# New planned latencies and six more matmuls on zeros in an attention and expert kernel with a planned order

## The chip, the cores and the metric

The kernel runs on one core of a Trainium2 chip. The metric is the device time of one execution in microseconds; the lower the better. Before the change three runs took 217.77, 216.84 and 217.11 us, a median of 217.11 us.

## What is computed

Two branches on the same 2048 x 512 input x, blended by a gate (cut from the reference; B = 1, S = 2048, D = 512):

```python
g = sigmoid((x * gate_w).sum(-1, keepdims=True))
# A: attention, 32 heads of 16, each query sees itself and the 255 keys before it
qkv = (x @ wqkv).reshape(B, S, 3, 32, 16).transpose(2, 0, 3, 1, 4)
scores = einsum("bhqd,bhkd->bhqk", q, k) * 16 ** -0.5
scores = where((i - j >= 0) & (i - j < 256), scores, -1e9)
a = einsum("bhqk,bhkd->bhqd", softmax(scores), v).transpose(0, 2, 1, 3).reshape(B, S, D) @ wo
# B: the 8 tokens with the largest r go through a gated feed-forward layer
r = x @ w_r;  idx = argsort(-r)[:8];  x_sel = x[idx]
y = ((silu(x_sel @ w_gate) * (x_sel @ w_up)) @ w_down) * sigmoid(r[idx])
b = x.at[idx].add(y)
out = g * a + (1 - g) * b
```

w_gate and w_up are 512 x 1792, w_down is 1792 x 512. All inputs are bf16.

## The kernel before

**Tiling.** The 32 heads are four groups c of eight, the 2048 keys four blocks qb of 512. That gives 16 steps s = 4c + qb. A step's scores are 16 key tiles of 32 keys by up to 288 queries, written as one stream of columns and cut into blocks of 512 columns. Such a block, for two halves of 64 partitions, is called a unit here; there are 136. For each unit TensorE writes scores into one of two PSUM pairs (`L717`), ScalarE takes the exponential into P (`L731`), and VectorE clears what lies outside the window (`L752`, for every second unit). TensorE then multiplies P by the values, which stand next to a column of ones in `Vbd` (`L771`), so that the sum of the exponentials comes out beside the result.

**The normalization of a step.** VectorE copies the two PSUM banks to `OXY` (`L800`), which frees the banks. Four small transfers bring the sums to `Dc` (`L805`), VectorE takes their reciprocal (`L812`), a transfer writes it to memory (`fs_r`, `L813`), another reads it back spread over the partitions (`f_Rb`, `L814`), and GpSimd multiplies (`L815`) into OT. `OXY` has three buffers, `Dc` and `Rb` two. The last two steps do it with transposes on TensorE instead (`norm_t`, `L823` to `L848`).

**Around it.** Projections of Q and K (`L582`) and of V (`L606`) are spread between the units. V goes to memory (`fs_v`, `L618`) and is read back in the layout of `Vbd` (`L622`). The routing scores come from `L860`, the feed-forward layer is `L896` to `L958`; its three weights follow each other in the same buffer `f_WF` (`L532`, `L913`, `L942`, each some 1.6 to 1.8 MB), and its result is scattered into a copy of x in memory (`fs_xc`), of which the last group of heads reads its residual (`resid`, `L629` and `L633`). The output product is `L663`, and `L650` with `L656` for the last block of rows.

**What sets the order.** The program is a list of operations with what they read and write. `Sched.schedule` plays it through with an estimated duration for each and, for each transfer, an estimated latency `lat` (2200 ns where none is given). At every step each engine takes, of its operations that are ready by these estimates, the one of the best priority. The result is a fixed order for each engine; on the chip every engine runs its list strictly in that order and waits at an instruction whose inputs are late. Nearly all transfers are issued by SyncE, in one such list. PSUM banks 4 to 7 are handed out in the same play-through. The estimate of when an input is there is this:

```python
if d.dma:
    x = d.t1 + d.lat + 100.0
elif sem:
    x = d.t1 + (70.0 if d.eng == op.eng else self.SEM) + (60.0 if d.eng == "pe" else 0.0)
```

At the head TensorE multiplies zeros into the eight banks (`L539`) while the input is on its way.

## Time and profile before

| | |
|---|---|
| median of three runs | 217.11 us |
| profiled execution | 218.79 us, of it 216.1 us from the first to the last instruction |
| TensorE busy | 169.8 us (79%) |
| VectorE busy | 145.6 us (67%) |
| ScalarE busy | 128.7 us (60%), of it 126.7 us in the 136 exponentials |
| GpSimd busy | 26.4 us (12%) |
| mean granted TensorE clock | 0.906 |

The shares are means over stages that differ: in the middle of the program all engines stand still together several times. The times of the profiled execution add up to its own 218.79 us, which is 1.68 us above the median. Where an engine waits, the trace names the instruction whose semaphore came last, and that is not always where the delay began.

### The profile page before, as it was taken

What the parts mean: (1) busy time and instruction counts of PE and PEld (TensorE: products, weight loads), DVE (VectorE), ACT (ScalarE), POOL (GpSimd) and SP (SyncE); (2) the same over time, 40 slices, a digit from 0 to 9 for tenths busy, and PEclk for the clock granted to TensorE, in tenths of its full rate; (3) what the DMA queues carried; (4) which work ended last, traced back from release to release, by engine and by line L of the source; (5) the groups of instructions that cost most, each with busy time, mean ns of one, the idle gap of its engine ahead of it and who ended that gap; (6) DMA issues with size and microseconds to landing.
All of it is one profiled execution on the core that took longest, in us unless ns stands there. A gap on an engine that the chain in (4) does not pass through costs nothing. (4 is left out here: it accounts for less than half of the span.)

```text
span 216.1 us, 6692 instructions
## 1 busy us (share of the span) xinstructions
PE 169.8 (79%) x2884; PEld 85.9 (40%) x2884; DVE 145.6 (67%) x365; ACT 128.7 (60%) x142; POOL 26.4 (12%) x42
## 2 busy tenths in 40 slices
PE   6699978999059938529898876998988898799930
PEld 1545535444025413215543633653443554534310
DVE  8289999782086398344754758376896866798870
ACT  2019999799017929708283494789969999500000
POOL 8300000100200202022003000202102022220000
PEclk9799999999655988967999996799999999999985
DMA  7997967497965617931477567256121213203841
GB/s 163 237 232 177 208 145 153 90 317 231 249 266 156 258 40 215 245 84 52 141 171 189 133 229 150 55 173 136 55 79 33 79 34 80 72 36 118 294 146 35
DMA packets 53058, 32.17 MB, mean 149 GB/s; under 512 B 37736, under 2 KB 49276, under 8 KB 52992
## 3 DMA queue, kind: packets, MB, share of 16 engines
q1 hardware_dynamic: 51376, 31.16, 53.7%
q10 hardware_dynamic: 1584, 0.52, 1.1%
q8 instruction: 23, 0.38, 0.7%
q14 instruction: 11, 0.09, 0.2%
q0 software_dynamic: 64, 0.02, 0.0%
HBM read 20.20 MB, written 9.42 MB: 137 GB/s over the span
## 5 line engine op out<-in xcount | busy, mean ns | idle before, releaser
L731 ACT ACTIVATE f_P<-f_ps 128x1024 bf16<-128x1024 f32 (+1 forms) x136 | 126.7, 1058 | 55.8 <-PE f_ps L717 29.6
L717 PE MATMUL f_ps<-f_QT,f_Kst 64*128 64x288 bf16 (+5 forms) x744 | 55.1, 252 | 9.8 <-ACT f_P L731 9.2
L771 PE MATMUL f_ps<-f_P,f_Vbd 64*34 64x288 bf16 (+8 forms) x1408 | 48.2, 262 | 4.6 <-DVE f_OXY L800 2.5
L752 DVE TENSOR_TENSOR f_P<-f_P,f_MK 128x512 bf16<-128x512 bf16 (+4 forms) x102 | 37.6, 388 | 15.5 <-ACT f_P L731 15.0
L582 PE MATMUL f_ps<-f_XT,f_W 64*128 64x512 bf16 x256 | 38.9, 389 | 3.0 <-DMA f_XT<-in_A_x_dram 2.4
L717 PEld LDWEIGHTS f_ps<-f_QT,f_Kst 64*128 64x128 bf16 x744 | 22.7, 96 | 41.3 <-ACT f_P L731 34.0
L771 PEld LDWEIGHTS f_ps<-f_P,f_Vbd 64*34 64x34 bf16 x1408 | 27.5, 98 | 27.1 <-issue 16.4
L815 POOL TENSOR_TENSOR f_OT<-f_OXY,f_Rb 128x512 bf16<-128x512 f32 x14 | 17.8, 1270 | 134.3 <-DMA f_Rb<-fs_r 134.3
L606 PE MATMUL f_ps<-f_W,f_XT 64*128 64x256 bf16 x256 | 22.0, 305 | 8.0 <-DVE f_zbf L925 6.4
L812 DVE RECIPROCAL f_RC<-f_Dc 128x32 f32<-128x32 f32 x14 | 4.9, 348 | 23.6 <-DMA f_Dc<-f_OXY 23.6
L800 DVE COPY f_OXY<-f_ps 128x512 f32<-128x512 f32 x28 | 18.3, 681 | 2.9 <-PE f_ps L771 2.9
L596 DVE TENSOR_SCALAR f_Kst<-f_Kr,f_hm 128x512 bf16<-128x512 bf16 x64 | 18.5, 345 | 0.0
L606 PEld LDWEIGHTS f_ps<-f_W,f_XT 64*128 64x128 bf16 x256 | 13.2, 106 | 13.0 <-DVE f_zbf L925 6.7
L582 PEld LDWEIGHTS f_ps<-f_XT,f_W 64*128 64x128 bf16 x256 | 11.0, 96 | 11.1 <-issue 3.5
L613 DVE CAST f_Vn<-f_ps 128x512 bf16<-128x512 f32 x16 | 10.7, 685 | 6.9 <-PE f_ps L606 6.8
L592 DVE CAST f_Kr<-f_ps 128x512 bf16<-128x512 f32 x16 | 10.9, 682 | 5.5 <-PE f_ps L582 5.5
L663 PE MATMUL f_ps<-f_wo,f_OT 64*128 64x512 bf16 x96 | 11.9, 378 | 0.2
L637 DVE SCALAR_TENSOR_TENSOR f_outt<-f_ps,f_g_f,f_xr 128x512 bf16<-128x512 f32 x16 | 11.2, 742 | 0.9 <-PE f_ps L663 0.9
L587 DVE CAST f_QT<-f_ps 128x512 bf16<-128x512 f32 x16 | 10.9, 681 | 0.0
L909 PE MATMUL f_ps<-f_WF,f_xselT 128*32 128x448 bf16 x32 | 2.8, 484 | 10.2 <-DVE f_Kr L592 10.2
L633 DVE TENSOR_SCALAR f_xr<-f_xr,f_omg_f 128x512 bf16<-128x512 bf16 x16 | 4.9, 348 | 5.0 <-DMA f_xr<-fs_xc 5.0
L1031 ACT COPY f_sg<-f_ones_f 1x1 f32<-1x1 f32 x1 | 0.2, 190 | 10.7 <-DVE flag L1027 10.7
(87 smaller groups left out, 75.4 us busy)
## 6 DMA issues: line engine op xcount, KB each, us to landing
fs_v<-f_Vn SPq DMA_DIRECT2D x8, 608.0 KB, 4.2
f_Vbd<-fs_v SPq DMA_DIRECT2D x32, 144.0 KB, 4.7
f_Rb<-fs_r SPq DMA_DIRECT2D x14, 256.0 KB
f_xr<-fs_xc SPq DMA_DIRECT2D x4, 512.0 KB
out_dram<-f_outt SPq DMA_DIRECT2D x16, 128.0 KB
f_OXY<-f_OXY SPq DMA_DIRECT2D x28, 64.0 KB, 2.8
f_WF<-in_B_w_gate_dram SPq DMA_DIRECT2D x1, 1792.0 KB
f_WF<-in_B_w_up_dram SPq DMA_DIRECT2D x1, 1792.0 KB
```

What stands on the lines that cost most here:

```text
L582: return e.matmul(ps[:, bk.i, :], W[R, k, f0:f0 + 128], XT[R, k, 512 * tc:512 * tc + 512], start=first, stop=last, tile_position=(64 * h, ...
L587: S.add("dve", lambda e: e.tensor_copy(out=QT[:, c % 2, 512 * tc:512 * tc + 512], in_=ps[:, bk.i, :]), r=[("bk", id(bk))], w=[("QT", c % 2 ...
L596: S.add(eng, lambda e, j=j: e.tensor_scalar(out=Kst[:, s, :, j, :], in0=Kr[:, n % 2, :].rearrange("p (a k) -> p a k", k=32), scalar1=hm[:, ...
L606: return e.matmul(ps[:, bk.i, 256 * i:256 * i + 256], XT[R, kc, 128 * a:128 * a + 128], W[R, kc, 1024 + 256 * cp:1024 + 256 * cp + 256], s ...
L637: S.add("dve", lambda e: e.scalar_tensor_tensor(out=outt[:, a % 4, :], in0=ps[:, bk.i, :], scalar=g_f[:, a:a + 1], in1=xr[:, (a // 4) % 2, ...
L663: return e.matmul(ps[:, bk.i, :], OT[R, k, 128 * a:128 * a + 128], wo[R, k, :], start=first, stop=last, tile_position=(64 * h, 0), skip_gr ...
L717: ins = e.matmul(ps[:, sbk + v, so:so + m], Kst[R, ks, t, :, :].rearrange("p j k -> p (j k)"), QT[R, c % 2, q0:q0 + m], start=True, stop=T ...
L731: S.add("act", lambda e, p0=p0, n=n, sbk=sbk: e.activation(out=P[:, g, :, p0:p0 + n], in_=ps[:, sbk:sbk + 2, 0:n], func=ACT.Exp, scale=0.2 ...
L752: S.add("dve", lambda e, v=v, m=m: e.tensor_tensor(out=v, in0=v, in1=m, op=ALU.min), r=rd, w=[("M", g, r_[3]) for r_ in b], dur=60 + 2 * k ...
L771: ins = e.matmul(ps[64 * v:64 * v + 34, bk.i, q0:q0 + n], Vbd[R, cp, kh, 36 * q:36 * q + 34], P[R, g, v, PADW + o:PADW + o + n], start=fir ...
L800: S.add("dve", lambda e, b=b, bk=bk: e.tensor_copy(out=OXY[:, x, b, :], in_=ps[:, bk.i, :]), r=[("O", id(bX))], w=[("OXY", x, b, p) for p ...
L815: S.add("pool", lambda e: e.tensor_tensor(out=OT[:, c, 512 * qb:512 * qb + 512], in0=OXY[:, x, 0, :], in1=Rb[:, y, :], op=ALU.mult), r=[(" ...
```

## The change

It changes numbers that the planner reads, and the list of matmuls on zeros. Nothing is computed otherwise, and no operation but the six matmuls is added or removed.

```diff
-                        x = d.t1 + (70.0 if d.eng == op.eng else self.SEM) + (60.0 if d.eng == "pe" else 0.0)
+                        x = d.t1 + (70.0 if d.eng == op.eng else self.SEM) + ((160.0 if op.eng == "pe" else 60.0) if d.eng == "pe" else 0.0)
...
-        for b in list(range(8)):
+        for b in list(range(8)) + [4, 5, 6, 7, 4, 5]:
             S.add("pe", lambda e, b=b: e.matmul(ps[:, b, :], zb[:, 0:128], zb, start=True, stop=True), r=[("xr", 0)], w=[("warm", b)] + ([("S", b // 2)] if b < 4 else []), dur=430, prio=0,
...
                     S.dma(lambda e: e.dma_start(vs[cp, 512 * tc:512 * tc + 512, :].rearrange("(i p) f -> p i f", p=128), Vn[:, s2]),
-                          r=[("Vn", s2, 0), ("Vn", s2, 1)] + [("Vn1", s2, j) for j in range(4)], w=[("vs", cp, tc)], prio=14)
+                          r=[("Vn", s2, 0), ("Vn", s2, 1)] + [("Vn1", s2, j) for j in range(4)], w=[("vs", cp, tc)], prio=14, lat=4500)
                         S.dma(lambda e, j=j, rj=rj: e.dma_start(Vbd[32 * j:32 * j + 32, cp, 16 * tc:16 * tc + 16, :],
                                                                 vs[cp, 512 * tc:512 * tc + 512, rj:rj + 144].rearrange("(a k) f -> k a f", k=32)),
-                              r=[("vs", cp, tc)], w=[("Vbd", cp, tc, j)], prio=14)
+                              r=[("vs", cp, tc)], w=[("Vbd", cp, tc, j)], prio=14, lat=4500)
             S.dma(lambda e: e.dma_start(xr[:, g], xc[512 * qb:512 * qb + 512, :].rearrange("(i p) f -> p i f", p=128)), r=["xc"],
-                  w=[("xr", g)] + [("xu", g, i) for i in range(4)], prio=30)
+                  w=[("xr", g)] + [("xu", g, i) for i in range(4)], prio=30, lat=6000)
...
         def pv_step(s):
             c, qb = s // 4, s % 4
+            LD = 7000 if s < 12 else 3000
...
                     S.dma(lambda e, h=h, b=b: e.dma_start(Dc[64 * h + 32 * b:64 * h + 32 * b + 32, y, :], OXY[32 + 64 * h:34 + 64 * h, x, b, :]),
-                          r=[("OXY", x, b, "d")], w=[("Dc", y, h, b)], prio=10)
+                          r=[("OXY", x, b, "d")], w=[("Dc", y, h, b)], prio=10, lat=LD)
...
-            S.dma(lambda e: e.dma_start(Rb[:, y, :], bass.AP(rs.tensor, s * 4096, [[512, 8], [0, 16], [1, 512]])), r=[("rs", s)], w=[("Rb", y)], prio=10, lat=3200)
+            S.dma(lambda e: e.dma_start(Rb[:, y, :], bass.AP(rs.tensor, s * 4096, [[512, 8], [0, 16], [1, 512]])), r=[("rs", s)], w=[("Rb", y)], prio=10, lat=LD + 1000)
...
-            S.dma(lambda e: e.dma_start(gz[:], gs.rearrange("(a p) -> p a", p=128), allow_slow_non_contiguous=True), r=["gs"], w=["gz"], prio=40, lat=4000)
+            S.dma(lambda e: e.dma_start(gz[:], gs.rearrange("(a p) -> p a", p=128), allow_slow_non_contiguous=True), r=["gs"], w=["gz"], prio=40, lat=9000)
```

From `pv_step` on, lines of the changed kernel are one higher (`L812` becomes `L813`).

What that does to the orders is shown at three places. VectorE, from the copies of step 1 to its reciprocal, before:

```order
L800 COPY f_OXY<-f_ps 128x512
L752 TENSOR_TENSOR f_P<-f_P,f_MK 128x2x4x64
L800 COPY f_OXY<-f_ps 128x512
L592 CAST f_Kr<-f_ps 128x512
L752 TENSOR_TENSOR f_P<-f_P,f_MK 128x2x4x64
L596 TENSOR_SCALAR f_Kst<-f_Kr,f_hm 128x16x32 x2
L752 TENSOR_TENSOR f_P<-f_P,f_MK 128x2x64
L596 TENSOR_SCALAR f_Kst<-f_Kr,f_hm 128x16x32 x2
L587 CAST f_QT<-f_ps 128x512
L752 TENSOR_TENSOR f_P<-f_P,f_MK 128x2x32 x7
L812 RECIPROCAL f_RC<-f_Dc 128x32
L752 TENSOR_TENSOR f_P<-f_P,f_MK 128x2x4x64 x2
```

VectorE in the changed kernel, the last rows up to the reciprocal of the same step; its copies (`L801`) stand 25 and 23 rows of this list ahead of it:

```order
L871 TENSOR_SCALAR f_eg<-f_eg 128x16
L901 CAST f_xselT<-f_ps 128x128
L872 RECIPROCAL f_g_f<-f_eg 128x16
L884 CAST f_sgf<-f_sgb 1x8
L873 CAST f_g_bf<-f_g_f 128x16
L874 CAST f_g_f<-f_g_bf 128x16
L752 TENSOR_TENSOR f_P<-f_P,f_MK 128x2x4x64
L875 TENSOR_SCALAR f_omg_bf<-f_g_bf 128x16
L877 CAST f_omg_f<-f_omg_bf 128x16
L752 TENSOR_TENSOR f_P<-f_P,f_MK 128x2x4x64
L592 CAST f_Kr<-f_ps 128x512
L813 RECIPROCAL f_RC<-f_Dc 128x32
```

Between the second copy and the reciprocal stand 15 instructions before and 31 now; the reciprocal has moved behind the first two masks of step 4. Counted in units whose masks stand ahead, the later copy and the reciprocal of steps 0 to 5 stand after 17 and 22, 29 and 34, 38 and 43, 42 and 47, 49 and 56, 63 and 67 units before, and after 15 and 27, 27 and 38, 38 and 47, 45 and 58, 52 and 63, 63 and 68 now. The first eight operations on the residual (`L633`) stand after 72 to 77 units before and 85 to 95 now.

SyncE where the first feed-forward weight (`f_WF<-in_B_w_gate_dram`) and the sums of the first steps are moved, before:

```order
L532 DMA f_WF<-in_B_w_gate_dram 128x4x1792
L618 DMA fs_v<-f_Vn 128x4x608
L813 DMA fs_r<-f_RC 128x32
L515 DMA f_W<-in_A_wqkv_dram 128x4x256
L622 DMA f_Vbd<-fs_v 32x16x144
L814 DMA f_Rb<-fs_r 128x1x512
L622 DMA f_Vbd<-fs_v 32x16x144 x3
L885 DMA f_sigT<-f_sgf 8x1x1
L805 DMA f_Dc<-f_OXY 32x1x32 x4
```

SyncE at the same place in the changed kernel:

```order
L869 DMA f_gz<-fs_g 128x16x1
L532 DMA f_WF<-in_B_w_gate_dram 128x4x1792
L806 DMA f_Dc<-f_OXY 32x1x32 x4
L622 DMA f_Vbd<-fs_v 32x16x144 x4
L618 DMA fs_v<-f_Vn 128x4x608
L515 DMA f_W<-in_A_wqkv_dram 128x4x128
L885 DMA f_idxT<-f_idxu 8x1x1
L515 DMA f_W<-in_A_wqkv_dram 128x4x128
L515 DMA f_W<-in_A_wqkv_dram 128x4x256
L944 DMA f_outt<-in_B_w_down_dram 112x2x512
L810 DMA f_OXY<-f_OXY 32x512 x2
L806 DMA f_Dc<-f_OXY 32x1x32
```

The first weight is now issued ahead of the sums of step 0, and nine rows stand between it and the first sum of step 1; before, the sums of step 1 stood behind the weight and behind the reads into `Vbd`, which wait for `fs_v`.

SyncE around the third weight (`f_WF<-in_B_w_down_dram`), before:

```order
L942 DMA f_WF<-in_B_w_down_dram 112x14x512
L805 DMA f_Dc<-f_OXY 32x1x32 x3
L814 DMA f_Rb<-fs_r 128x1x512
L805 DMA f_Dc<-f_OXY 32x1x32
L809 DMA f_OXY<-f_OXY 32x512 x2
L813 DMA fs_r<-f_RC 128x32
L814 DMA f_Rb<-fs_r 128x1x512
L805 DMA f_Dc<-f_OXY 32x1x32 x4
```

SyncE at the same place in the changed kernel:

```order
L806 DMA f_Dc<-f_OXY 32x1x32 x4
L810 DMA f_OXY<-f_OXY 32x512 x2
L814 DMA fs_r<-f_RC 128x32
L806 DMA f_Dc<-f_OXY 32x1x32 x2
L943 DMA f_WF<-in_B_w_down_dram 112x14x512
L815 DMA f_Rb<-fs_r 128x1x512
L810 DMA f_OXY<-f_OXY 32x512 x2
L814 DMA fs_r<-f_RC 128x32
L806 DMA f_Dc<-f_OXY 32x1x32 x2
```

The four sums of step 4 are now issued ahead of the third weight, and half of those of step 5; its other half stands behind the weight.

On TensorE 13 matmuls on zeros come first, then the first pair of V projections, the last matmul on zeros, a second pair of V, and then Q and K; before, two Q and K matmuls went ahead of the first V pair. The first product of P with the values of a step stands after 12, 20, 31, 40, 48, 51 and 67 units for steps 0 to 6 (before after 9, 25, 32, 40, 42, 55 and 67); the second feed-forward product (`L910`) after 60 units (`L909` before: 49), the third (`L952`) after 74 (`L951` before: 68). For steps 6 to 14 these numbers are the same in both, for step 15 they are 130 before and 132 now. At the end one copy of step 14, the reciprocal of step 13 and two of the rounds of transposes, reciprocals and products have moved behind the last mask.

## Rows read from the trace of the kernel before

**Rows 1.** The waits, whole span: engine, line, releaser; us in total, times, longest us
```profile
ACT f_P L731 <- PE f_ps L717: 29.6, 14, 11.8
...
ACT f_P L731 <- PE f_ps L771: 25.9, 7, 10.3
...
DVE f_RC L812 <- DMA f_Dc<-f_OXY: 23.6, 7, 9.5
...
PE f_ps L909 <- DVE f_Kr L592: 10.2, 2, 6.6
...
DVE f_xr L633 <- DMA f_xr<-fs_xc: 5.0, 4, 2.0
```

**Rows 2.** VectorE timeline, four reciprocals: start us, us, instruction [idle before <-releaser]
```profile
39.42 0.35 DVE L812 RECIPROCAL f_RC<-f_Dc 128x32 f32<-128x32 f32 x1 [1.57 <-DMA f_Dc<-f_OXY]
...
59.43 0.35 DVE L812 RECIPROCAL f_RC<-f_Dc 128x32 f32<-128x32 f32 x1 [9.49 <-DMA f_Dc<-f_OXY]
...
75.23 0.35 DVE L812 RECIPROCAL f_RC<-f_Dc 128x32 f32<-128x32 f32 x1 [3.59 <-DMA f_Dc<-f_OXY]
...
94.91 0.35 DVE L812 RECIPROCAL f_RC<-f_Dc 128x32 f32<-128x32 f32 x1 [6.52 <-DMA f_Dc<-f_OXY]
```

**Rows 3.** SyncE timeline, 40 to 94 us: when transfers were issued
```profile
40.55 1.51 SPq L532 DMA_DIRECT2D f_WF<-in_B_w_gate_dram  x1
...
42.10 0.51 SPq L618 DMA_DIRECT2D fs_v<-f_Vn  x1
...
51.51 0.32 SPq L622 DMA_DIRECT2D f_Vbd<-fs_v  x1
...
54.90 2.62 SPq L805 DMA_DIRECT2D f_Dc<-f_OXY  x4
...
66.81 0.40 SPq L913 DMA_DIRECT2D f_WF<-in_B_w_up_dram  x1
...
67.26 2.66 SPq L805 DMA_DIRECT2D f_Dc<-f_OXY  x4
...
82.69 0.35 SPq L942 DMA_DIRECT2D f_WF<-in_B_w_down_dram  x1
...
83.14 3.42 SPq L805 DMA_DIRECT2D f_Dc<-f_OXY  x3
...
93.11 1.20 SPq L809 DMA_DIRECT2D f_OXY<-f_OXY  x2
```

**Rows 4.** Busy time by stretch (columns in the first row)
```profile
core 0: us, PE busy (x) PEld busy (x) DVE busy (x) ACT busy (x) POOL busy (x), PEclk, DMA share, GB/s
15.66:54.00 38.34, 35.12 (x636) 17.74 (x632) 30.71 (x82) 35.97 (x41) 1.08 (x1) 1.00 0.75 189
54.00:131.20 77.20, 54.05 (x926) 27.88 (x926) 44.56 (x104) 42.18 (x45) 8.50 (x7) 0.84 0.60 171
61.00:69.20 8.20, 7.32 (x142) 4.16 (x146) 5.53 (x12) 3.42 (x4) 0.00 (x0) 0.50 0.55 194
131.50:137.50 6.00, 6.00 (x80) 3.34 (x84) 3.21 (x9) 3.02 (x3) 0.47 (x1) 0.50 0.72 142
160.00:186.70 26.70, 23.59 (x589) 12.76 (x575) 19.34 (x52) 26.56 (x29) 3.80 (x3) 1.00 0.24 67
```

**Rows 5.** TensorE timeline, the head of the program
```profile
1.24 3.55 PE L539 MATMUL f_ps<-f_xr 128*128 128x512 bf16 x8 [1.24 <-DVE f_hmi L476]
...
7.22 0.39 PE L582 MATMUL f_ps<-f_XT,f_W 64*128 64x512 bf16 x2 [2.43 <-DMA f_XT<-in_A_x_dram]
```

**Rows 6.** Busy time by stretch: the head and the tail
```profile
7.20:10.70 3.50, 3.48 (x36) 2.83 (x38) 0.00 (x0) 0.00 (x0) 0.00 (x0) 0.62 1.22 236
186.70:210.00 23.30, 19.11 (x163) 7.84 (x155) 20.68 (x59) 0.21 (x2) 2.63 (x3) 0.99 0.41 136
```

**Rows 7.** VectorE timeline, normalization of the last two steps
```profile
188.65 0.69 DVE L823 COPY f_OXY<-f_ps 128x512 f32<-128x512 f32 x1 [0.30 <-PE f_ps L771]
...
190.06 0.34 DVE L839 TENSOR_TENSOR f_On<-f_ps,f_RC 128x64 bf16<-128x64 f32 x2
```

## The prediction

> **What bounds the kernel now.** I read the waits first. ScalarE waits 29.6 us for score matmuls and 25.9 us more that the view books on the value product; VectorE waits 23.6 us at seven of its 14 reciprocals for the sums `Dc`; TensorE waits 10.2 us ahead of the feed-forward product for a copy on VectorE [rows 1]. These are one chain. VectorE runs its list in order, so while it stands at a reciprocal it empties no PSUM bank and masks nothing; TensorE then has no bank, ScalarE gets no scores. The VectorE timeline has the four large waits: 1.57, 9.49, 3.59 and 6.52 us, 21.17 in all [rows 2].
>
> The SyncE timeline says why the sums are late, and it is twice not the transfer itself. At 42.10 us `fs_v` is issued right behind the first weight; the first read into `Vbd`, which needs it, goes out at 51.51, and until then nothing else can. The sums of step 1 are therefore issued at 54.90 to 57.52 and release the reciprocal at 59.43. For step 2 they are issued at 67.26 to 69.92, just behind the second weight (66.81), and land at 75.23. For step 4 the third weight goes out at 82.69, three of the sums behind it at 83.14 to 86.56, and the next transfer that needs them leaves at 93.11 [rows 3].
>
> The busy times by stretch give the size. From 15.66 to 54.00 us TensorE is busy 35.12 and ScalarE 35.97 of 38.34 us: both near full. From 54.00 to 131.20 they are busy 54.05 and 42.18 of 77.20. In 61.00 to 69.20, behind the longest pause, TensorE works 7.32 us at half its clock (granted 0.50), and again for 6.00 us from 131.50. From 160 on ScalarE is busy 26.56 of 26.70 us and sets the pace [rows 4].
>
> **The change part by part.** The sum is made against the profiled 218.79 us, 216.1 of them span; that is 1.68 above the median of 217.11, and I take the difference over to the median.
>
> *Six more matmuls on zeros.* Eight take 3.55 us, 0.44 each; then TensorE idles 2.43 us until the input lands at 7.22 [rows 5], and its next 36 matmuls run at a mean clock of 0.62 for 3.48 us [rows 6]. Thirteen take 5.8 us from 1.24, to 7.0: still under the input's arrival. The fourteenth stands between the V pairs, 0.2 to 0.4 us. If the clock stays up, 3.48 us at 0.62 become some 2.2 and give 1.3; less the fourteenth, about 1. Against it V goes first, but the first Q and K pair was already split by both V pairs. I take -0.7; bounds -1.2 and +0.4 (clock as before).
>
> *Longer latency for `Dc`, `Rb`, `fs_v`, `Vbd` and the gate.* This moves the reciprocals back on VectorE. For step 1 there are 31 instructions instead of 15 behind the copy, and the masks of eleven units rather than five. A unit takes ScalarE 0.88 us (35.97 / 41, [rows 4]), so the reciprocal comes some 10 us after the copy. The wait of 9.49 us before came from SyncE's stand between 42.61 and 51.51 in front of the read into `Vbd`, with one small issue in it [rows 3]. That stand goes too: in the new list the first weight is issued before the sums of step 0, and the reads that need the last `fs_v` stand behind the sums of step 1. What is late next is step 0 behind the first weight: its reciprocal stands twelve units behind its copy, 10.6 us, and a weight and the sums behind it take 8 to 10 us to land (66.81 to 75.23; 82.69 to 93.11, [rows 3]); 0 to 1 us is left. So for 15.66 to 54.00 I take -1.2, the wait of 1.57 less a rest; bounds -2 and +1.
>
> *The stretch 54.00 to 131.20.* Without waits TensorE needs 54.05 us less the half-clock loss in 61.00 to 69.20, 7.32 / 2 = 3.66: 50.4. At the share of 0.916 that it reached from 15.66 to 54.00 (35.12 / 38.34) that is 55.0 us; ScalarE, with 42.18, isn't the limit. So with every wait gone the stretch could give 22.2. They don't all go. Work runs closer together, the three weights and the copy of x take the queues as long as before (8 to 10 us each), and I find four places where the sums still stand behind one: step 2 behind the copy of x, step 3 behind the second weight (its reciprocal 13 units after its copy), step 4 behind a read of `fs_r` that waits for the same weight, and the second half of step 5 behind the third weight (reciprocal five units after that copy, though in a stretch where TensorE is behind). I put these at 1, 1, 1 and 2 us: 5.2 together, taken near the smallest wait of rows 2 since each misses by little. That gives -17. Bounds: -25 (every wait gone, and the other low clocks too) and -7 (half of the 21.17 comes back, with the slow clock behind it).
>
> *The residual.* VectorE waits 5.0 us four times for `f_xr` [rows 1]; in the new order these stand after 85 to 95 units instead of 72 to 77. Behind the old place TensorE ran 6.00 us at half clock, 3.0 us lost. I take -2.5; bounds -4 and +1. From 160 to 186.7 us ScalarE is full: 0.
>
> *The tail.* One copy of step 14 (0.69 us [rows 7]) and the last memory reciprocal (0.35 [rows 2]) move behind the last mask, and with them two of the eight rounds of the transposed normalization, each with two products (0.34 [rows 7]) and a short reciprocal. VectorE is busy 20.68 of the last 23.30 us [rows 6], so nothing hides them: +2; bounds 0 and +3.
>
> *The 100 ns more for a matmul that waits for a matmul* only moves work; its effect is in the orders above.
>
> Sum: -0.7 - 1.2 - 17 - 2.5 + 2 = -19.4. 218.79 - 19.4 = 199.4 for a profiled execution, 217.11 - 19.4 = 197.7 for the median. I say 198.
>
> **A rule that speaks against the change.** The sums of step 2 landed 5.3 us after their last issue, those of step 1 after 1.9 (59.43 less 57.52) [rows 2, 3]. The Trainium skill (DMA: Bandwidth & Descriptors, section Anatomy of one DMA) has a cost of some 2.0 us plus bytes at 436 GB/s, fitted on GpSimd's path. By it sums of 4 KB land after 2 us, and a planned latency of 7 us would be 5 too long. The trace agrees with it for step 1 and not behind a weight, and there the measurement decides. By the rule alone the waits of steps 2 and 4 would have been some 3 and 4 us shorter and the sum smaller by as much.
>
> **Rivals.**
> - *The bulk transfers follow the sums (chance 0.16).* The four rests are not 5 us but 13, since all transfers are pushed into a stretch 17 us shorter, where their share of the queues, 0.60 now, rises towards 0.77. For it: TensorE's place leaves only a unit or two of slack at each. Against it: TensorE itself needs 55 us there, which gives transfers time. Eight us more: 206.
> - *Planned too late (0.05).* With 7 us for the sums and 8 for `Rb` the plan thinks the three `OXY` buffers held for longer and puts copies, and so PSUM banks and the value products, later: step 4's products start after 48 units instead of 42, step 15's after 132 instead of 130. If each of the eleven steps from 4 to 14 paid the bank wait of such a shift, two units or 1.8 us, that would cost 19.8 and eat the gain: about 217. Against it: the products of steps 6 to 14 start at the same units as before.
> - *TensorE stands at a weight (0.07), the slower side.* The second and third feed-forward products are fixed after 60 and 74 units. Score matmuls queue behind them, ScalarE dries up after two units. The second weight is issued behind a read of `fs_r` that waits for the copy of x, the third behind the sums of step 5. Each such wait can cost a full landing of 10.4 us, and behind it half the clock on 7 to 8 us of work (3.7). Two of them, 28, less the 19.4: 226; it decides the sign from 19.4 us of waits on. Against it: the sums of step 5 are copied from unit 58 on, so the third weight has 16 units, over 14 us. One of the two alone gives 212. Of the 0.07 I give 0.05 to both.
>
> **How the numbers follow.** The forecast, up to some 204 us, has 0.72; the rivals 0.16 (206), 0.05 (217) and 0.07 (212 or 226). 0.5%, 1.1 us, is about what can be told from no change. Faster by more: 0.72 + 0.16 and the 0.02 of a single weight, 0.90; within: 0.04, most of the plan that is too late; slower: the 0.05 of two weights and 0.01 of the late plan, 0.06. The likeliest case alone runs from 191 (all but a little of the 25 gained) to 204. For eight in ten I take 190 to 209, which takes in the first rival and leaves out the two last and a little below.
>
> **What would show it.** The wait of VectorE for `Dc` falls from 23.6 to about 5 us, and no single one is over 4. ScalarE's exponential of unit 83, now at 131 us, is done by some 112. No stretch of low clock longer than 3 us behind unit 40. The first exponential starts at about 15.0 instead of 15.66. The stretch from the last exponential to the last output instruction is 2 us longer. The forecast is wrong if the waits for `Dc` stay over 12 us, if the second or third feed-forward product shows a wait of several us for `f_WF`, or if the waits go and TensorE's busy share from unit 39 to 83 stays under 0.8.

## The result and the profile after

The changed kernel takes 199.43 us (median of 4 executions, 198.81 to 199.86) where the kernel before took 217.44 (217.11 in the runs of the prediction): a ratio of 0.918, with an interval of 0.914 to 0.922. The profiled execution took 199.66 us, 196.9 of them span; its mean granted clock is 0.965, before 0.906. Where the executions of a kernel spread by more than 1.5%, a ratio goes by its faster ones, so that it need not be the quotient of the two medians.

The waits of the whole span, after (engine, line, releaser; us in total, times, longest); they answer to [rows 1]:

```profile
ACT f_P L731 <- PE f_ps L771: 16.7, 5, 7.2
ACT f_P L731 <- PE f_ps L717: 16.3, 6, 11.2
DVE f_RC L813 <- DMA f_Dc<-f_OXY: 9.2, 3, 4.4
...
PE f_ps L663 <- POOL f_OT L816: 3.0, 1, 3.0
...
DVE f_xr L633 <- DMA f_xr<-fs_xc: 1.2, 1, 1.2
```

ScalarE's waits for TensorE fall from 55.5 to 33.0 us, 11.2 of them the start of the program; VectorE's for `Dc` from 23.6 to 9.2. The wait of 10.2 us ahead of the feed-forward product is gone. New is the wait of 3.0 us of TensorE for a product of GpSimd.

VectorE's reciprocals of steps 1 to 6 (start us, us, and in brackets the idle time before); they answer to [rows 2]:

```profile
52.52 0.34 DVE L813 RECIPROCAL f_RC<-f_Dc 128x32 f32<-128x32 f32 x1
62.77 0.35 DVE L813 RECIPROCAL f_RC<-f_Dc 128x32 f32<-128x32 f32 x1
72.79 0.35 DVE L813 RECIPROCAL f_RC<-f_Dc 128x32 f32<-128x32 f32 x1
77.88 0.34 DVE L813 RECIPROCAL f_RC<-f_Dc 128x32 f32<-128x32 f32 x1
90.08 0.35 DVE L813 RECIPROCAL f_RC<-f_Dc 128x32 f32<-128x32 f32 x1 [3.56 <-DMA f_Dc<-f_OXY]
106.26 0.35 DVE L813 RECIPROCAL f_RC<-f_Dc 128x32 f32<-128x32 f32 x1 [4.36 <-DMA f_Dc<-f_OXY]
```

The reciprocals of steps 1, 2 and 4, which cost 19.60 us, wait for nothing. Steps 5 and 6 wait. SyncE's issues say why; they answer to [rows 3]:

```profile
53.43 2.67 SPq L806 DMA_DIRECT2D f_Dc<-f_OXY  x4
...
61.42 0.46 SPq L914 DMA_DIRECT2D f_WF<-in_B_w_up_dram  x1
...
73.19 2.59 SPq L806 DMA_DIRECT2D f_Dc<-f_OXY  x4
...
79.22 0.34 SPq L943 DMA_DIRECT2D f_WF<-in_B_w_down_dram  x1
...
82.75 1.37 SPq L806 DMA_DIRECT2D f_Dc<-f_OXY  x2
89.65 0.62 SPq L815 DMA_DIRECT2D f_Rb<-fs_r  x1
90.32 1.01 SPq L618 DMA_DIRECT2D fs_v<-f_Vn  x2
95.41 0.32 SPq L622 DMA_DIRECT2D f_Vbd<-fs_v  x1
...
101.52 2.67 SPq L806 DMA_DIRECT2D f_Dc<-f_OXY  x4
```

The sums of steps 2 and 4 now go out ahead of the second and third weight. The second half of step 5 stands behind the third weight: its last issue ends at 84.12 and the reciprocal is released at 90.08, 6.0 us later. The sums of step 6 go out late for the old reason in a new place: their copies are done at 92.85, but the read into `Vbd` waits until 95.41 for the `fs_v` issued at 90.32, and the sums queue behind it until 101.52. That `fs_v` is itself late: the data of both its transfers were ready by 85.62, but SyncE stood 5.4 us, until 89.65, at a read (`f_Rb`) of the `fs_r` that went out at 82.12, behind the third weight. That write was ready to be read 7.0 us after its issue, the one before it (77.17) after at most 1.9. So here too the weight stands near the start of the chain. The sums end at 104.19 and release the reciprocal 2.1 us later. The Trainium skill (DMA: Bandwidth & Descriptors, section Anatomy of one DMA) has about 2.0 us plus bytes at 436 GB/s for a transfer that GpSimd issues; step 6 agrees with it, though SyncE issues its sums, and step 5, which landed behind a weight, does not.

SyncE's stands have moved rather than gone: its waits at reads into `Vbd` fall from 19.5 to 6.7 us in the whole span, those at reads of `fs_r` rise from 10.7 to 17.9. What has changed is that fewer reciprocals wait behind them.

Busy time by stretch, after; these answer to [rows 4] and [rows 6]:

```profile
core 0: us, PE busy (x) PEld busy (x) DVE busy (x) ACT busy (x) POOL busy (x), PEclk, DMA share, GB/s
15.05:51.90 36.85, 34.52 (x644) 17.66 (x640) 31.93 (x84) 35.97 (x41) 1.10 (x2) 1.00 0.90 216
51.90:107.10 55.20, 47.93 (x918) 24.45 (x914) 38.31 (x93) 41.01 (x45) 8.48 (x7) 1.00 0.67 194
107.10:134.50 27.40, 23.66 (x458) 12.59 (x458) 21.30 (x57) 22.21 (x24) 2.99 (x2) 0.94 0.73 184
107.10:110.50 3.40, 2.27 (x34) 1.25 (x38) 3.40 (x9) 0.06 (x1) 0.00 (x0) 0.63 1.00 282
134.50:162.60 28.10, 24.13 (x618) 12.65 (x614) 18.73 (x46) 26.44 (x29) 3.81 (x3) 1.00 0.19 50
162.60:196.90 34.30, 21.26 (x163) 9.31 (x160) 22.43 (x68) 0.23 (x2) 3.84 (x4) 0.85 0.37 114
```

The bounds are the same events as before: the first exponential, units 39, 83, 107 and 136, and the end of the span. Before, these stood at 15.66, 54.0, 131.2, 158.4, 186.7 and 216.1.

| stretch | before | after | difference | foretold |
|---|---|---|---|---|
| start to first exponential | 15.66 | 15.05 | -0.6 | -0.7 |
| to unit 39 | 38.3 | 36.9 | -1.5 | -1.2 |
| to unit 83 | 77.2 | 55.2 | -22.0 | -17 |
| to unit 107 | 27.2 | 27.4 | +0.2 | -2.5 |
| to unit 136 | 28.3 | 28.1 | -0.2 | 0 |
| to the end of the span | 29.4 | 34.3 | +4.9 | +2 |

The sum is -19.2, that of the prediction -19.4: the forecast of 198 is met within 1.5 us, but by terms that miss by up to 5 and cancel; that it is so close is in part luck.

At the head (answers to [rows 5]) TensorE's timeline has thirteen matmuls on zeros and then V:

```profile
1.24 5.11 PE L539 MATMUL f_ps<-f_xr 128*128 128x512 bf16 x13 [1.24 <-DVE f_hmi L476]
7.00 1.05 PE L606 MATMUL f_ps<-f_W,f_XT 64*128 64x256 bf16 x16 [0.66 <-DMA f_XT<-in_A_x_dram]
```

### The profile page after: what moved, and what is told of

Same layout as the page of the kernel before. It is cut to its first block, busy times and chain, and to the rows that moved or that the text cites. A ratio compares the mean times of both kernels' runs of the same rounds, so it can differ in the third digit from the quotient of the medians.

```text
span 196.9 us, 6699 instructions
## 1 busy us (share of the span) xinstructions
PE 164.1 (83%) x2889; PEld 82.5 (42%) x2890; DVE 142.8 (72%) x365; ACT 127.3 (65%) x142; POOL 26.8 (14%) x42
## 5 line engine op out<-in xcount | busy, mean ns | idle before, releaser
L731 ACT ACTIVATE f_P<-f_ps 128x1024 bf16<-128x1024 f32 (+1 forms) x136 | 125.3, 1081 | 33.1 <-PE f_ps L771 16.7
L717 PE MATMUL f_ps<-f_QT,f_Kst 64*128 64x288 bf16 (+5 forms) x744 | 53.4, 244 | 9.6 <-ACT f_P L731 8.9
L752 DVE TENSOR_TENSOR f_P<-f_P,f_MK 128x512 bf16<-128x512 bf16 (+4 forms) x102 | 34.4, 355 | 24.4 <-ACT f_P L731 23.7
L771 PE MATMUL f_ps<-f_P,f_Vbd 64*34 64x288 bf16 (+8 forms) x1408 | 46.9, 251 | 4.6 <-DVE f_OXY L801 3.0
L582 PE MATMUL f_ps<-f_XT,f_W 64*128 64x512 bf16 x256 | 37.0, 376 | 1.2 <-DVE f_QT L587 0.9
L771 PEld LDWEIGHTS f_ps<-f_P,f_Vbd 64*34 64x34 bf16 x1408 | 25.7, 94 | 26.2 <-issue 17.7
L816 POOL TENSOR_TENSOR f_OT<-f_OXY,f_Rb 128x512 bf16<-128x512 f32 x14 | 18.1, 1299 | 105.3 <-DMA f_Rb<-fs_r 105.3
L606 PE MATMUL f_ps<-f_W,f_XT 64*128 64x256 bf16 x256 | 17.8, 269 | 1.4 <-DMA f_XT<-in_A_x_dram 0.7
L801 DVE COPY f_OXY<-f_ps 128x512 f32<-128x512 f32 x28 | 18.2, 675 | 0.0
L663 PE MATMUL f_ps<-f_wo,f_OT 64*128 64x512 bf16 x96 | 13.5, 399 | 3.2 <-POOL f_OT L816 3.0
L606 PEld LDWEIGHTS f_ps<-f_W,f_XT 64*128 64x128 bf16 x256 | 11.5, 94 | 5.5 <-DVE f_QT L587 1.4
L592 DVE CAST f_Kr<-f_ps 128x512 bf16<-128x512 f32 x16 | 10.7, 671 | 3.6 <-PE f_ps L582 3.6
L813 DVE RECIPROCAL f_RC<-f_Dc 128x32 f32<-128x32 f32 x14 | 4.8, 345 | 9.2 <-DMA f_Dc<-f_OXY 9.2
L637 DVE SCALAR_TENSOR_TENSOR f_outt<-f_ps,f_g_f,f_xr 128x512 bf16<-128x512 f32 x16 | 11.3, 745 | 0.2
L663 PEld LDWEIGHTS f_ps<-f_wo,f_OT 64*128 64x128 bf16 x96 | 4.2, 97 | 9.0 <-POOL f_OT L816 3.1
L539 PE MATMUL f_ps<-f_xr 128*128 128x512 bf16 x14 | 5.5, 564 | 1.2 <-DVE f_hmi L476 1.2
```

Source lines behind the costliest of these rows:

```text
L582: return e.matmul(ps[:, bk.i, :], W[R, k, f0:f0 + 128], XT[R, k, 512 * tc:512 * tc + 512], start=first, stop=last, tile_position=(64 * h, ...
L606: return e.matmul(ps[:, bk.i, 256 * i:256 * i + 256], XT[R, kc, 128 * a:128 * a + 128], W[R, kc, 1024 + 256 * cp:1024 + 256 * cp + 256], s ...
L637: S.add("dve", lambda e: e.scalar_tensor_tensor(out=outt[:, a % 4, :], in0=ps[:, bk.i, :], scalar=g_f[:, a:a + 1], in1=xr[:, (a // 4) % 2, ...
L663: return e.matmul(ps[:, bk.i, :], OT[R, k, 128 * a:128 * a + 128], wo[R, k, :], start=first, stop=last, tile_position=(64 * h, 0), skip_gr ...
L717: ins = e.matmul(ps[:, sbk + v, so:so + m], Kst[R, ks, t, :, :].rearrange("p j k -> p (j k)"), QT[R, c % 2, q0:q0 + m], start=True, stop=T ...
L731: S.add("act", lambda e, p0=p0, n=n, sbk=sbk: e.activation(out=P[:, g, :, p0:p0 + n], in_=ps[:, sbk:sbk + 2, 0:n], func=ACT.Exp, scale=0.2 ...
```

## The experiments

All ratios are to the kernel before on the same chip, 220.2 to 220.5 us there. The first four runs were on one chip, the next four on a second, the last four on a third. The changed kernel itself ran on the second alone: 200.15 us, 0.908 by the medians, where the result above has 0.918. On the other two a difference to it is one between ratios, and it is given for both. An edit of a latency changes the whole plan, so each run shows what one plan did and not the price of one number.

**The longer latency of the sums alone** (the kernel before, with one part of the change):

```diff
+            LD = 7000 if s < 12 else 3000
-  ... w=[("Dc", y, h, b)], prio=10)
+  ... w=[("Dc", y, h, b)], prio=10, lat=LD)
-  ... w=[("Rb", y)], prio=10, lat=3200)
+  ... w=[("Rb", y)], prio=10, lat=LD + 1000)
```

> The kernel before with only the longer planned latency of the sums and of their way back (7 and 8 us, from step 12 on 3 and 4). Theory A (the gain comes from the reciprocals' place): the waits for Dc fall from 23.6 to 6-12 us and the time to 200-206. Theory B (the gain comes from SyncE's list, by the latencies of fs_v and Vbd): the stand in front of Vbd behind the first weight stays, and with it 8 us or more of waiting; 209-214.

Measured: 213.25 us, 0.967 (0.961 to 0.973). The waits for `Dc` fall to 6.3 us, lower than in the changed kernel, and yet the time falls by 6.9 us and not by 20. TensorE now waits 3.3 us for the second weight itself, VectorE 6.4 us for the residual, and ScalarE is idle 4 to 5 us each ahead of units 51, 57, 66 and 80:

```profile
DVE f_RC L813 <- DMA f_Dc<-f_OXY: 6.3, 3, 3.5
...
PE f_ps L910 <- DMA f_WF<-in_B_w_up_dram: 3.3, 1, 3.3
```

From unit 39 to 83 it takes 67.7 us, 9.5 less than before, and its tail is 32.5, 3.1 more. SyncE still stands 5.8 us in front of `Vbd` behind the first weight, as theory B had it, but no long wait of a reciprocal follows. So theory A had the waits right and not the time, theory B the time and not the waits. The wait at the reciprocals alone is not the gain.

**All but that latency** (the changed kernel, the three edits above undone):

> The changed kernel with the latency of the sums and of their way back as before (2.2 and 3.2 us), all else as changed. Theory A: reciprocals close behind their copies again, waits for Dc 15-22 us, time 210-215. Theory B: SyncE's list does it alone, waits under 10 us, 200-205.

Measured: 210.06 us, 0.943 (0.934 to 0.953). The waits for `Dc` are 17.7 us in six pieces, the largest 7.28 and 4.76. Theory A holds, at the low end of its time. So the rest of the change brings 10 to 12 us without it, and this latency some 5 to 10 on top of the rest.

**The weights shrunk, both orders.** The first two weights move an eighth and the third a seventh of their bytes, in the kernel before and in the changed one; the buffer is set to zero once on GpSimd. The feed-forward part therefore computes on incomplete weights.

```diff
+        S.add("pool", lambda e: e.memset(WF1[:], 0.0), w=["wg"], dur=6000, prio=60)
-  e.dma_start(WG, B_w_gate.rearrange("(k p) f -> p k f", p=128))
+  e.dma_start(WG[:, :, 0:224], B_w_gate.rearrange("(k p) f -> p k f", p=128)[:, :, 0:224])
...
-  e.dma_start(WDv, wdv[:, 0:14, :])
+  e.dma_start(WDv[:, 0:2, :], wdv[:, 0:2, :])
```

> The kernel before, its orders unchanged, but each of the three feed-forward weights is moved only in part (two of the three an eighth, the third a seventh; the rest of the buffer is zeroed once at the start on GpSimd), so the feed-forward branch computes with the rest as zero. If the sums were late because they queue behind those weights: waits for Dc under 8 us, no wait over 4, time 197-204. If they were late by SyncE's own list and the fixed time of a transfer: waits above 15 us, 211 or more.

> The changed kernel, its orders unchanged, with the same partly moved weights (the rest zero). If its remaining 9.2 us of waits for Dc are what is left of the queue behind the weights: under 3 us, time 190-195. If TensorE or the copy of x sets the pace there: waits stay at 5 or more, 196-200. The difference to the kernel before with such weights is what the new orders are worth without the bulk: 0-6 us by theory A, 12 or more if the orders gain something else.

Measured: 207.65 us (0.940, 0.934 to 0.947) with the orders of before, and 198.16 us (0.895, 0.889 to 0.901) with the new ones. The waits for `Dc` with the orders of before:

```profile
DVE f_RC L812 <- DMA f_Dc<-f_OXY: 12.3, 7, 3.6
```

and with the new orders:

```profile
DVE f_RC L813 <- DMA f_Dc<-f_OXY: 1.0, 1, 1.0
```

Half of the 23.6 us of waits before, 11.3, was the bytes of the weights on the queues. The other half stays with the small weights, between the two theories, and SyncE's list has a part in it still: it stands 6.7 us, until 62.82, at a read of an `fs_r` that went out behind the copy of x in memory (issued at 52.85). The sums of step 2, copied by 59.05, go out behind that stand at 64.03, and their reciprocal waits 3.55 us. The new orders are still worth 9.5 us without the weights, again between the two theories; their waits are under 3 us, as the first had it, but the time is not 190 to 195.

One thing disturbs the pair: the zeroing on GpSimd delays the first exponential, to 16.41 us with the orders of before (15.66) and to 18.40 with the new ones (15.05), so the second kernel loses 2.6 us more at its head than the first. Its idle time of ScalarE ahead of units 66 and 73, 4.45 and 6.38 us, is about as large as in the changed kernel (4.44 and 7.22): that remainder is not a matter of the weights' bytes. In the changed kernel TensorE shows what it is:

```profile
80.14 1.91 PE L582 MATMUL f_ps<-f_XT,f_W 64*128 64x512 bf16 x14
81.88 2.15 PE L606 MATMUL f_ps<-f_W,f_XT 64*128 64x256 bf16 x32
83.96 1.43 PE L771 MATMUL f_ps<-f_P,f_Vbd 64*34 64x32 bf16 x56
```

```profile
84.27 6.31 ACT L731 ACTIVATE f_P<-f_ps 128x1024 bf16<-128x1024 f32 x7 [4.44 <-PE f_ps L771]
97.80 9.27 ACT L731 ACTIVATE f_P<-f_ps 128x1024 bf16<-128x1024 f32 x10 [7.22 <-PE f_ps L771]
```

ScalarE waits there for the value product (`L771`), and ahead of that product TensorE works through projections of Q, K and V without a pause. Ahead of unit 73 it is the same with the third feed-forward product (`L952`) and two groups of V projections, from 91.80 until the value product at 97.49. These waits are TensorE's own work, in the order that the plan gave it.

**The changed kernel once more**, on the chip of the next three:

> The changed kernel once more, unaltered, so that the three kernels beside it have their comparison on the same chip. Both theories: a ratio to the kernel before of 0.918 give or take 0.005, with 9 us of waits at the reciprocals, one of over 4 us ahead of unit 83, and 34 us from the last exponential to the end of the span.

Measured: 200.15 us (195.45 to 200.42, six runs), a ratio of 0.908 by the medians and not 0.918. The same orders fell differently in this execution: the waits for `Dc` are 3.2 us and not 9.2, there is no idle time ahead of unit 83, and units 83 to 107 take 23.4 us instead of 27.4. Unit 39 is done 3.6 us later, part of it behind a wait of 1.89 us of TensorE for the gathered row and at a granted clock of 0.50 from 48.4 to 55.2. The tail is 34.1 us. The span is 197.5 against 196.9. So the two waits of 3.56 and 4.36 us that the first profile shows are no fixed cost of the order, and the time does not follow their sum.

**The tail's orders.**

```diff
-            LD = 7000 if s < 12 else 3000
+            LD = 7000 if s < 9 else 3000
```

> The longer planned latency holds only for steps 0 to 8 instead of 0 to 11; the orders up to unit 99 stay word for word, and at the end one copy, one memory reciprocal and one pair of products come back ahead of the last mask. Theory C (the tail is 4.9 us longer because the plan put work of VectorE and GpSimd behind the last mask): the stretch from the last exponential to the end falls from 34 to 30 or 31 us, TensorE no longer waits 3 us for a copy of GpSimd into f_OT, and the time is 3 to 4 us under the unaltered changed kernel. Theory D (the exponentials now come 24 us earlier, and VectorE and GpSimd have the same backlog whatever their order): the tail stays at 33 to 35 us and the time within 1 us.

Measured: 195.84 us (192.50 to 197.42, six runs) against 200.15 for the unaltered one beside it; the means differ by 4.0 us, give or take some 2.4 worked out from the spread of the two sixes, and the quickest of each by 3.0. The tail is 29.5 us, against 34.1 and 34.3 in the two traces of the changed kernel. The waits from the last exponential on, in the changed kernel:

```profile
POOL f_OT L816 <- DMA f_Rb<-fs_r: 13.6, 2, 9.2
...
PE f_ps L663 <- POOL f_OT L816: 3.0, 1, 3.0
```

and in this one:

```profile
POOL f_OT L816 <- DMA f_Rb<-fs_r: 8.8, 2, 5.9
...
PEld f_ps L663 <- POOL f_OT L816: 0.7, 1, 0.7
```

Theory C holds: here TensorE's wait for GpSimd (`L816`) is down to 0.5 us, 0.7 on its weight loads (PEld). GpSimd's timeline shows where it waited in the changed kernel,

```profile
165.14 2.49 POOL L816 TENSOR_TENSOR f_OT<-f_OXY,f_Rb 128x512 bf16<-128x512 f32 x2 [9.21 <-DMA f_Rb<-fs_r]
```

two products in a row, for steps 11 and 12, after a wait of 9.21 us, and TensorE's output products behind them,

```profile
166.46 1.89 PE L663 MATMUL f_ps<-f_wo,f_OT 64*128 64x512 bf16 x8 [3.03 <-POOL f_OT L816]
...
174.06 1.28 PE L663 MATMUL f_ps<-f_wo,f_OT 64*128 64x512 bf16 x8
```

the first eight of which then take 1.89 us where eight later ones take 1.28. This version is faster than both kernels, 0.888 of the kernel before by the medians.

**The residual's scalings back in their place.**

```diff
-  w=[("xr", g)] + [("xu", g, i) for i in range(4)], prio=30, lat=6000)
+  w=[("xr", g)] + [("xu", g, i) for i in range(4)], prio=30)
```

> The planned latency of the residual's reads goes back to what it was; only VectorE's order differs, by the 13 scalings of f_xr, which come about 5 to 10 units earlier. Theory of the prediction (later scalings save 2.5 us of waits and of slow clock): VectorE waits 4 to 5 us for f_xr and the time is 2 to 3 us over the unaltered changed kernel. Rival (the scalings were late only because the weights were ahead of them, and now either place is after the landing): waits for f_xr under 2 us and the time within 0.7 us.

Measured: 202.04 us (200.74 to 204.03), 1.9 over the unaltered kernel beside it by the medians, and every one of the six runs is slower than every run of that one. VectorE's wait,

```profile
DVE f_xr L633 <- DMA f_xr<-fs_xc: 6.7, 3, 3.3
```

is 3.3 us in the unaltered one. The rival is out. The prediction's theory holds in direction, with more wait than it gave and somewhat under its 2.5 us of time; the size is not sharp, since the runs of each kernel spread by 3 to 5 us.

**The added zeros made short.**

```diff
-        for b in list(range(8)) + [4, 5, 6, 7, 4, 5]:
-            ... e.matmul(ps[:, b, :], zb[:, 0:128], zb, start=True, stop=True)
+        for wn, b in enumerate(list(range(8)) + [4, 5, 6, 7, 4, 5]):
+            ... n = 512 if wn < 8 else 32: e.matmul(ps[:, b, 0:n], zb[:, 0:128], zb[:, 0:n], start=True, stop=True)
```

> The six added matmuls on zeros have 32 columns instead of 512 and do next to nothing; the orders are the same. Theory of the prediction (the added zeros hold the clock up for the first projections): TensorE's granted clock from 7.0 to 10.7 us falls from 1.00 to about 0.6, V, K and Q take about 1.3 us longer, and the first exponential and the time come 0.5 to 1.0 us later. Rival (behind the projections the copies on VectorE set the pace): the clock falls all the same, but the first exponential and the time move by under 0.3 us.

Measured: 200.65 us (199.56 to 202.36), 0.5 over the unaltered one by the medians. The stretch behind the zeros, short and then as changed:

```profile
7.00:10.70 3.70, 3.50 (x33) 2.48 (x35) 0.00 (x0) 0.00 (x0) 0.15 (x1) 0.55 1.15 249
```

```profile
7.00:10.70 3.70, 3.63 (x45) 2.17 (x47) 1.29 (x2) 0.00 (x0) 0.16 (x1) 1.00 1.19 246
```

The granted clock falls from 1.00 to 0.55, 33 matmuls are done instead of 45, and the first exponential comes at 16.62 us instead of 15.05 (15.55 in the repeat): 1.1 to 1.6 us. At the head the zeros do what was foretold and somewhat more (0.5 to 1.0), and the rival's 0.3 is out; how much of it reaches the end, 0.5 us by the medians and 1.4 by the means, these runs don't resolve.

**The 100 ns on TensorE undone.**

```diff
-  ((160.0 if op.eng == "pe" else 60.0) if d.eng == "pe" else 0.0)
+  (60.0 if d.eng == "pe" else 0.0)
```

> The changed kernel, but an operation of TensorE that waits for a matmul is planned 60 ns behind it again, not 160. Nothing else is edited; the second feed-forward product then stands after 66 units instead of 61, and reciprocals of steps 2 to 9 stand 2 to 7 units elsewhere. Theory of the prediction (the 100 ns only move work, the latencies are what gains): 0.918 of the kernel before give or take 0.012, waits for Dc of 3 to 12 us. Rival (a plan of TensorE that runs 100 ns too fast at every such step issues projections and products too early, and this term carries a good part of what the latencies leave): 0.935 or more, with TensorE idle more from unit 39 to 83.

Measured: 209.12 us, 0.947 (0.942 to 0.951): the rival. Waits for `Dc` are 6.8 us, but ScalarE is idle 5.92 us ahead of unit 41, 4.81 ahead of 66, 4.12 and 4.55 ahead of 86 and 90, and VectorE waits 8.1 us for the residual. From unit 39 to 83 this kernel takes 59.8 us, with TensorE busy for 0.82 of it (0.87 in the changed one), as the rival had it; from 83 to 107 it takes 33.4, 6.0 more, which neither theory named.

**The latency of V undone.**

```diff
-  ... w=[("vs", cp, tc)], prio=14, lat=4500)
+  ... w=[("vs", cp, tc)], prio=14)
...
-  r=[("vs", cp, tc)], w=[("Vbd", cp, tc, j)], prio=14, lat=4500)
+  r=[("vs", cp, tc)], w=[("Vbd", cp, tc, j)], prio=14)
```

> The changed kernel, but writes of V to memory and the reads into Vbd are planned as short as before. Theory A (a read into Vbd that stands on SyncE in front of sums is one of the two causes of late sums, and only this latency moves it): SyncE stands again at a read into Vbd for 3 us or more between 40 and 75 us, a reciprocal of step 0 to 4 waits 3 us or more, and the time is 0.93 to 0.945 of the kernel before. Theory B (with the longer latency of the sums alone the reciprocals are far enough back): no reciprocal up to step 4 waits over 2 us, and 0.918 give or take 0.012.

Measured: 218.40 us, 0.989 (0.985 to 0.992): nearly all the gain is gone, far more than theory A gave. A reciprocal waits 3.76 us at 55.85, as A had it, but SyncE does not stand at `Vbd` ahead of it, and the large loss is elsewhere. SyncE in this kernel:

```profile
38.49 0.51 SPq L532 DMA_DIRECT2D f_WF<-in_B_w_gate_dram  x1
...
40.19 6.59 SPq L515 DMA_DIRECT2D f_W<-in_A_wqkv_dram  x1
46.83 2.54 SPq L622 DMA_DIRECT2D f_Vbd<-fs_v  x3
...
52.54 1.96 SPq L806 DMA_DIRECT2D f_Dc<-f_OXY  x3
54.54 0.69 SPq L885 DMA_DIRECT2D f_idxT<-f_idxu  x1
```

and TensorE:

```profile
64.70 0.26 PE L897 MATMUL f_ps<-f_ident,f_xsel 64*128 64x32 bf16 x4 [13.45 <-DMA f_xsel<-in_A_x_dram,f_idxT]
```

The index of the chosen rows is ready on VectorE at 39.17 us, but its 32-byte transfer (`idxT`) is listed behind the reads into `Vbd` and the sums and goes out at 54.54; in the changed kernel it went out at 39.81. SyncE waits for next to nothing in between (0.4 us from 36 to 56): it is busy issuing, 6.59 us of it one read of `f_W`. GpSimd gathers the rows only then (56.58), right behind the copy of x (55.93), and the gather lands after 8.0 us, where it took 3.7 in the changed kernel. The four matmuls on what was gathered, fixed in TensorE's order, hold everything behind them for 13.45 us. Then TensorE runs at a mean clock of 0.55 from 60 to 72 us. It is the issuing order again, with another victim.

**V projections earlier**, on the kernel with the shorter tail, by 12 units and by 6:

```diff
-  work.append((U0(2 * cp, tc) - 8 if (cp, tc) != (0, 0) else -1, 1, "v", cp, tc))
+  work.append((U0(2 * cp, tc) - 8 - 12 * cp if (cp, tc) != (0, 0) else -1, 1, "v", cp, tc))
```

> On the kernel with the shorter tail (longer latency of the sums for steps 0 to 8 only), the second half's four V projections are allowed and made urgent 12 units earlier, so that they no longer stand between the parts of the third feed-forward product at unit 74. Theory E (from unit 60 to 83 TensorE is the bound only because V and the third product meet there; earlier there is room): the idle time of ScalarE ahead of units 66 and 73, 14 us before, falls to 8 or less, unit 83 is done 2 to 4 us earlier, and the time is 0.87 to 0.885 of the kernel before. Theory F (TensorE is full from unit 20 on, and moved work only moves the pause): the idle time comes back around units 41 to 60 and the time is 0.885 to 0.90.

> As the kernel with V 12 units earlier, but 6 units: V then stands after 48, 56, 58 and 66 units, and the last pair behind the third product. Theory E: idle time ahead of units 66 and 73 of 8 us or less, 0.87 to 0.885 of the kernel before. Theory F: 0.885 to 0.90, as without the move.

Measured: 205.5 us (0.931, 0.927 to 0.936) and 201.53 us (0.916, 0.911 to 0.920); of the first, one of six executions took 489.25 us, for which no cause was found. Both are slower than the kernel they start from (195.84), and neither theory gave that. Ahead of units 66 and 73 ScalarE is idle 11.8 us with 12 units and 8.2 with 6, so E fails, with 6 units by little in the idle time and plainly in the time; F has the pause elsewhere, which is seen (8.35 us ahead of unit 57; 8.93 ahead of unit 71), but at a higher price than it allowed. With 6 units TensorE's row is

```profile
97.85 1.87 PE L952 MATMUL f_ps<-f_WF,f_xr 112*8 112x512 bf16 x4 [7.49 <-DMA f_WF<-in_B_w_down_dram]
```

and SyncE's

```profile
84.78 0.44 SPq L943 DMA_DIRECT2D f_WF<-in_B_w_down_dram  x1
85.27 5.71 SPq L806 DMA_DIRECT2D f_Dc<-f_OXY  x4
```

The third weight now goes out 5.6 us later than in the changed kernel (79.22), while its product stands after 70 units and not 74: the prediction's third rival, TensorE at a weight. The four sums behind it took 5.71 us to issue, not 2.6 to 2.7, and their reciprocal waited 8.85 us.

The longer latency of the gate (`gz`) was not undone by itself; what it does in the plan is not shown.

## Why the prediction was right, and where it was not

*The chain.* That VectorE's stand at the reciprocals, behind SyncE's order and the weights, starves TensorE and ScalarE was right as to where the time went: from unit 39 to 83 that wait fell from 19.9 to 7.9 us and the stretch by 22.0. With the weights shrunk, half of the whole wait goes without any change of order, and with the new orders nearly all. But the wait has no fixed price, as the prediction's sum gives it one. With the longer latency of the sums alone it is smaller still, 6.3 us in all, and the stretch gives 9.5: TensorE then waits for the second weight, and ScalarE dries up at other units. The gain is that of the whole new order and not of this wait alone. One reading of the prediction is off: SyncE's stand before `Vbd` ran from 43.70 to 51.51, 7.8 us, with two small issues ahead of it and not one.

*The stretch to unit 83, the largest term: -22.0 for -17.* Two sizes were off, by about half of the 5 us each. TensorE's work was put at 50.4 us, with the low clock taken out of one window alone; the clock was 1.00 throughout and the work 47.93 us, which at the share of 0.916 is 52.3 us instead of 55.0. And "5.2 together" was added for waits (the four that it lists make 5.0). The share came out at 0.868, so 2.9 us is all that the waits and the crowding at units 66 and 73 cost there against 0.916. Of the four named places three wait for nothing; the fourth, behind the third weight, waited 3.56. The repeat, with 3.2 us of waits in all, needs 56.4 us for this stretch, 50.0 of them with TensorE busy. So the waits that are left do not set the time there; that TensorE's work does, as the prediction had it, fits the rows at units 66 and 73.

*The residual, +0.2 for -2.5.* The term itself stands: undone, it costs some 1.9 us. What failed is the list of late sums, which ended at step 5. The sums of step 6 stood behind a read that waits for `fs_v`, the very pattern of step 1 before, and `fs_v` behind a read that waited for a write behind the third weight; the reciprocal waited 4.36 us, TensorE 2.53 us behind it, and in the 3.4 us from 107.1 the mean clock was 0.63. Where that wait was 1.79 us and not 4.36, in the repeat, the same stretch took 23.4 us, 3.7 less than before.

*The tail, +4.9 for +2.* Counting VectorE's moved instructions was too little. `Rb` planned some 5 us later also put GpSimd's products and their reads late, and TensorE waited 3.03 us for them; the clock from the last exponential on was 0.85, before 0.89. With the shorter latency for steps 9 to 11 the tail is 29.5 us, as before the change (29.4).

*The head, -0.6 for -0.7*, but from two sizes that were off: the zeros are worth 1.1 to 1.6 us there, put at 1, and about 1.0 is lost again (16.62 with short zeros, 15.66 before), put at 0.3. The loss is not in V ahead of Q and K: with short zeros the first Q and K are done at 14.64, before at 14.75. It comes behind them, where TensorE now waits 0.50 us for VectorE's copy of Q and then spends 1.05 us on V ahead of the first scores, before 0.66.

*"The 100 ns more ... only moves work"* is wrong as a reason to leave it out of the sum. Without it the same latencies give 6 to 9 us less. The prediction lost nothing by this, since it read the finished orders. But a sum over edits would have: taking out the sums' latency, V's, or the 100 ns costs 5 to 10, 16 to 18 and 6 to 9 us, by which ratio is taken for the changed kernel (0.918 or 0.908). That is 27 to 37 together, in a change that is worth 18 to 20. In each of the three something else is late.

*The signs foretold.* Unit 83 was done at 107 (by 112), the first exponential at 15.05 (15.0), TensorE's share there is 0.87 (over 0.8), no feed-forward product waited for a weight. The waits for `Dc` were 9.2 us, not 5, and one was over 4; a low clock stood behind unit 83 and in the tail. The first rival, 13 us of rests and 206, did not come: the time is 199.43, and waits of 9.2 or 3.2 us leave the span within 0.6 us. The second, a plan that is too late and 217, came only at the tail, for the 4.9 us there. The third appears only in other plans.

What stays open: whether another order would spare the 11 to 14 us for which ScalarE is idle ahead of units 66 and 73 in every run with these orders there, since moving V away from there made it worse by other waits; and what the price of each latency is apart from the plan it happens to produce.

## What to carry to other kernels

Where the engines' orders are fixed ahead, follow every in-order queue, the issuing one too, through the whole program, and list each small transfer behind something that waits: a list that ends at the last wait of the trace before misses those that move. Do not add up edits to a planner: read the finished order, because a plan half corrected can be as slow as one not corrected. Keep a longer latency to the stretch where transfers are late; at the end of the program, where nothing hides the moved work, it cost 4 us here.

## What the runs showed of the hardware

An issue is not always short: four sums took SyncE 2.6 to 2.7 us, but 5.71 right behind the third weight in one run, and one read of `f_W` behind the first weight 6.59 us in another, in which SyncE issued nothing else. It need not be so: right behind the second weight, in the kernel before, four sums took 2.66. Sums released their reciprocal some 2 us after their last issue with no weight just ahead (1.9 for step 1 before, 2.1 for step 6 now), and 5.3 to 7.9 us after it behind a weight. Two executions of one program with the same orders differed by 6 us in their waits at reciprocals (9.2 and 3.2) and by 0.6 us in span. And an early task on GpSimd alone, the zeroing of a buffer, moved the first exponential from 15.05 to 18.40 us, although on the other engines the order was the same (with the orders of before, 15.66 to 16.41). The trace shows where. VectorE's preparation of the masks, in the changed kernel and then with the zeroing, is

```profile
2.02 4.98 DVE L488 TENSOR_SCALAR f_MK<-f_xi,f_kf 128x32 bf16<-128x32 f32 x2
```

```profile
2.03 11.22 DVE L488 TENSOR_SCALAR f_MK<-f_xi,f_kf 128x32 bf16<-128x32 f32 x2
```

With the zeroing, which runs from 7.12 to 13.18 us, it ends at 13.24, together with the two copies of V behind it, and TensorE waits 1.73 us for these copies. In both runs with the zeroing VectorE's row ends so. Why the one holds up the other no run here shows.
